# Sliding-window attention and a highway layer on one Trainium2 core: another order of loads and steps, and the gate's bias written at another place

## The chip, the core and the metric

The kernel runs on one core of a Trainium2 chip. The core has five engines that run at the same time, each with its own queue of instructions taken in order: TensorE (PE, matmuls; its weight loads are shown as PEld), VectorE (DVE), ScalarE (ACT), GpSimd (POOL) and SyncE (SP). Data comes from and goes to the chip's memory by DMA; here GpSimd issues nearly all loads and SyncE the stores. Matmul results go to PSUM, everything else is in SBUF. The metric is device time of one execution in microseconds (us), as a median of several.

## The reference

Attention with a window of 128 positions and 4 sink positions for 4 batches, 8 heads, 768 positions and a head size of 64; its output, 3072 tokens of 512 features, goes through a highway layer with two 512 x 512 weights.

```python
scores = scale * np.matmul(q, k.transpose(0, 1, 3, 2))
keep = is_sink | in_window          # pos < 4, or 0 <= query - key < 128
a = softmax(np.where(keep, scores, -1e9))
x = np.matmul(a, v)                 # then heads side by side: (3072, 512)
H = np.maximum(x @ w_h, 0.0)
T = 1.0 / (1.0 + np.exp(-(x @ w_t + b_t)))
out = T * H + (1.0 - T) * x
```

## The kernel before

**Blocks.** The 3072 tokens are 24 blocks of 128 queries, six to a batch. Keys and values are loaded in chunks of 128 that lie 64 positions off the query blocks, so block n needs key chunks n and n+1 (and n-1 for a corner) and the same of v. Chunks at a batch border are loaded in two halves.

**Steps.** Each step of a block has a short name, and the table ORDER lists them as `name:block`. All engines get their instructions in the order of this table, and what one step issues on an engine stays behind what earlier steps issued there.

- `Tq`, `Tk` (PE, L322): transposes of q and k into PSUM; `tq`, `tk` (ACT, L327): copies to SBUF; `tkV`, `tqV` the same on DVE. From block 3 on `S` carries the transposes of later blocks itself, and from block 9 one ACT copy `tt` (L334) takes both.
- `S` (PE, L375 and L388): scores of a block in two halves. `x0_`, `x1_` (ACT, L397): exp of the halves, later `xx` (L402) of both. `m0_`, `m1_`, `mm` (DVE, L408): masks.
- `sk` (PE, L357) and `es` (ACT, L364): scores and exp of the sink keys.
- `A` (PE, L441, L458, L464): the value matmuls: corners in quadrants of 64 x 64, the diagonal, and the sinks. One PSUM tile `av` serves all blocks in turn.
- `xh` (DVE, L472 and L477): division by the softmax sum. `X` (PE, L491): transposes of xh, into a free part of `av`. `xT` (ACT) or `xTV` (DVE) (L496): the copy; it must be done before `A` of the next block.
- `Mh` (PE, L519) and `Mt` (PE, L507): 4 matmuls each of 512 columns for H and for T. `u` (ACT, L512): tanh. `d` (L525), `U` (L531), `e` (L536), `o` (L548) (DVE): the rest of the layer and the store. For blocks 21 and 22 the last sum is made by GpSimd (`x2_`, `oP`). Block 23 is done in two halves of 256 columns (`Ta`, `Ha`, `ua`, `da`, `ea`, `pa` and the same with b).
- `wA` are filler matmuls on zeros; `mz`, `ma`, `na`, `mc`, `fa`, `fb`, `fc`, `fd`, `cv` are one-time set-up steps on DVE.

**PSUM.** Scores of the first blocks and all single transposes share two buffers in turn. Mh, Mt and the sink scores share two banks `m0`, `m1`; the string M_BANKS says which is used next.

**The t bias.** It is a matmul of a row of ones with the bias. For blocks 0 to 7 it is one matmul of 128 rows and 512 columns in `Mt` (L504). T_BESIDE maps a block n to the block whose bias is written in `A` of block n: from n = 9 on, two matmuls in the quadrants (low, low) and (high, high) stand ahead of the corner matmuls, which use the other two quadrants (L436). A branch for n >= LATE, which cuts them into pieces, is not used, since LATE is 99.

**Loads.** q and k of the first blocks come through one pool of 8 buffers, those of block 9 on through `late_pool` of 3; v has a ring of 14 tiles, of which 9 are used once. The first loads are written out by hand; after that `do_A` issues v of block n+4, q and k of block n+6 behind `A` of block n. `fill_ks` and `sink_v` (sink keys and values of a batch; from batch 1 on GpSimd) are issued by the copy step of the batch's first k, so they stand in GpSimd's queue behind the loads of earlier `A` steps.

Of the kernel before, what the change touches and what calls it, by code (L numbers as in the profile page):

```python
# [8 lines left out]
FP16 = mybir.dt.float16  # L9
# [11 lines left out]
def kernel(  # L21
# [37 lines left out]
    AHEAD = 8  # L59

    const = ctx.enter_context(tc.tile_pool(name="const", bufs=1))
    late_pool = ctx.enter_context(tc.tile_pool(name="p_late", bufs=3))
    sd_pool = ctx.enter_context(tc.tile_pool(name="p_sd", bufs=AHEAD))
    qkT_pool = ctx.enter_context(tc.tile_pool(name="p_qkT", bufs=7))
    tt_pool = ctx.enter_context(tc.tile_pool(name="p_tt", bufs=5))
    e_pool = ctx.enter_context(tc.tile_pool(name="p_e", bufs=3))
# [20 lines left out]

    ctx.callback(close_s)
    HP = P // 2
    T_BESIDE = {9: 8, 10: 9, 11: 10, 12: 11, 13: 12, 14: 13, 15: 14, 16: 15, 17: 16, 18: 17, 19: 18, 20: 19, 21: 20, 22: 21, 23: 22}  # L90
    LATE = 99
    M0 = 9
    FIRST = 9
    NV = FIRST + 5
    NS4 = H * NSINK
    KW = NHP * P + 32
    EW = P + HP
    v_ring = [const.tile([P, VW], FP16, tag=f"v{i}", name=f"v{i}") for i in range(NV)]
# [10 lines left out]

    def load_q(n):  # L110
        b, c = divmod(n, NSC)
        qsd = (sd_pool if n < FIRST else late_pool).tile([P, H, D], FP16, tag="qsd", name="qsd")
        nc.gpsimd.dma_start(out=qsd, in_=q[b, :, c * P:(c + 1) * P, :].transpose([1, 0, 2]))  # L113
        q_sd[n] = qsd

    def load_k(n):
        ksd = (sd_pool if n < FIRST else late_pool).tile([P, H, D], FP16, tag="ksd", name="ksd")
        for rows, b, s0 in chunk_parts(n):
            nr = rows.stop - rows.start
            nc.gpsimd.dma_start(out=ksd[rows], in_=k[b, :, s0:s0 + nr, :].transpose([1, 0, 2]))  # L120
# [69 lines left out]
    def load_w(w, sb):  # L190
        nc.gpsimd.dma_start(out=sb, in_=w.rearrange("(kc p) of -> p kc of", p=P))

    with tc.manual_schedule(engines={ENG.Pool, ENG.SP}):
        load_f32("q", 0, nc.sync)
        load_f32("k", 0, nc.scalar)
        load_f32("k", 1, nc.sync)
        load_f32("v", 0, nc.scalar)
        load_f32("v", 1, nc.sync)
        for r in (0, HP):
            nc.sync.dma_start(out=bt32[r:r + 1, :], in_=moe_b_t.unsqueeze(0))  # L200
        for b in range(B):
            nc.sync.dma_start(out=vs_dn[b], in_=v[b, :, 0:NSINK, :])
        nc.gpsimd.affine_select(
            out=ident, in_=ident, compare_op=ALU.is_equal, fill=0.0,
            base=0, pattern=[[-1, P]], channel_multiplier=1)
        tri(mask, slice(0, HP), 0, P, HP - 1, -1, 1)
        tri(mask, slice(HP, P), 0, P, 0, 1, -1)
        tri(mask, slice(0, HP), P, EW, 0, 1, -1)
        tri(mask, slice(HP, P), P, EW, -1, -1, 1)
        load_q(3)  # L210
        load_k(2)
        load_q(4)
        load_q(1)
        load_k(3)
        load_q(2)
        load_v(2)
        load_k(5)
        nc.gpsimd.affine_select(
            out=bm, in_=bm, compare_op=ALU.is_ge, fill=0.0,
            base=0, pattern=[[-NSINK, H]], channel_multiplier=1)  # L220
        nc.gpsimd.affine_select(
            out=bm, in_=bm, compare_op=ALU.is_ge, fill=0.0,
            base=NSINK - 1, pattern=[[NSINK, H]], channel_multiplier=-1)
        load_k(4)
        load_v(3)
        load_w(moe_w_h, wh_sb)
        load_q(5)
        load_k(6)
        load_w(moe_w_t, wt_sb)
        load_v(4)  # L230
        load_q(6)
        load_k(7)
        load_v(5)
        load_k(8)
        load_q(7)
        load_v(6)
        load_v(8)
        load_v(7)
# [33 lines left out]
    def sink_ones(_):  # L272
# [3 lines left out]

    m_bank = [m_ps.tile([P, DM], FP32, tag=f"m{i}", name=f"m{i}") for i in range(2)]
    M_BANKS = (
        "010101010101010101010101010010100101001100101011010110101101"
    )  # L280
    m_next = iter(M_BANKS)

# [329 lines left out]
    def on(n):  # L612
        return 0 <= n < NB
# [31 lines left out]
    def new_T(m, g):  # L645
        if g and m and m % NSC == 0 and m < NB:
            fill_ks(m // NSC, nc.gpsimd)
            sink_v(m // NSC, nc.gpsimd)

    def do_A(n):  # L650
        pe_A(n)
        if FIRST <= n + 4 <= NB:
            load_v(n + 4)
        if AHEAD <= n + 6 < NB:
            load_q(n + 6)
        if FIRST <= n + 6 <= NB:
            load_k(n + 6)

    def norm(n):
        dve_rec(n)  # L660
# [27 lines left out]
        "pa": lambda n: dve_half(n, 0, "o"), "pb": lambda n: dve_half(n, 1, "o"),  # L688
    }
    ORDER = """  # L690
    mz0_:0 ma:0 na:0 Tq:0 na:1 Tk:0 tq:0 mz1_:0 tk:0 ma:1 wA:0 wA:0 Tk:1 mc:0 cv:0 tk:1 fa:0
    wA:0 wA:0 wA:0 S:0 fb:0 x0_:0 cv:1 x1_:0 wA:0 wA:0 wA:0 wA:0 Tq:3 m0_:0 fc:0 tq:3 wA:0 Tk:2
    tk:2 m1_:0 fd:0 wA:0 wA:0 wA:0 wA:0 Tq:1 A:0 tq:1 S:1 xh:0 sk:1 x0_:1 x1_:1 Tq:2 m0_:1 X:0
    sk:3 xTV:0 es:1 Tk:3 m1_:1 tq:2 tk:3 wA:1 A:1 es:3 S:2 xh:1 x0_:2 x1_:2 Tk:4 m0_:2 sk:2
    tkV:4 X:1 es:2 m1_:2 S:3 xT:1 A:2 x0_:3 Mh:1 x1_:3 xh:2 tq:4 d:1 X:2 tk:5 Mh:0 xTV:2 m0_:3
    Mh:2 d:0 m1_:3 S:4 d:2 Mt:0 x0_:4 x1_:4 m0_:4 A:3 u:0 m1_:4 Mt:1 tq:5 xh:3 tk:6 U:0 sk:4 u:1
    e:0 S:5 es:4 o:0 X:3 x0_:5 U:1 sk:5 xTV:3 e:1 A:4 x1_:5 m0_:5 o:1 tq:6 Mt:2 tk:7 xh:4 es:5
    u:2 m1_:5 X:4 S:6 xT:4 U:2 e:2 A:5 x0_:6 o:2 Mh:3 x1_:6 xh:5 tq:7 Mh:4 m0_:6 tk:8 m1_:6 X:5
    d:3 S:7 xT:5 d:4 A:6 x0_:7 Mh:5 xh:6 x1_:7 Mt:3 d:5 tq:8 tk:9 m0_:7 X:6 u:3 m1_:7 Mt:5 xT:6
    U:3 e:3 sk:7 o:3 u:5 Tq:9 es:7 U:5 Mt:4 tq:9 e:5 o:5 S:8 u:4 U:4 A:7 x0_:8 e:4 o:4 Mt:6  # L700
    x1_:8 xh:7 tq:10 Mh:6 m0_:8 tk:10 m1_:8 u:6 X:7 d:6 S:9 xT:7 U:6 A:8 e:6 xx:9 o:6 sk:9 xh:8
    Mh:7 es:9 tt:9 mm:9 Mt:7 d:7 X:8 u:7 S:10 xTV:8 U:7 A:9 e:7 xx:10 o:7 Mt:8 xh:9 tt:10 Mh:8
    mm:10 u:8 X:9 d:8 S:11 xT:9 U:8 A:10 e:8 xx:11 o:8 sk:11 xh:10 Mt:9 es:11 tt:11 mm:11 Mh:9
    u:9 X:10 d:9 S:12 xT:10 U:9 A:11 e:9 xx:12 o:9 Mt:10 xh:11 tt:12 Mh:10 mm:12 u:10 X:11 d:10
    S:13 xT:11 U:10 A:12 e:10 xx:13 o:10 sk:13 xh:12 Mt:11 es:13 tt:13 mm:13 Mh:11 u:11 X:12
    d:11 S:14 xT:12 U:11 A:13 e:11 xx:14 o:11 Mh:12 xh:13 tt:14 Mt:12 mm:14 X:13 u:12 d:12 S:15
    xT:13 U:12 e:12 xx:15 A:14 o:12 sk:15 xh:14 Mt:13 tt:15 mm:15 es:15 X:14 S:16 u:13 xTV:14
    U:13 A:15 xx:16 Mh:14 xh:15 tt:16 Mt:14 d:14 mm:16 Mh:13 u:14 U:14 sk:17 d:13 X:15 es:17
    S:17 xT:15 e:13 e:14 A:16 xx:17 o:13 o:14 Mt:15 xh:16 tt:17 Mh:15 mm:17 u:15 X:16 S:18 d:15
    xT:16 U:15 A:17 xx:18 e:15 o:15 Mh:16 xh:17 tt:18 Mt:16 mm:18 X:17 u:16 S:19 xTV:17 d:16  # L710
    A:18 xx:19 U:16 e:16 sk:19 xh:18 Mt:17 es:19 mm:19 tt:19 Mh:17 o:16 u:17 X:18 S:20 xT:18
    d:17 U:17 A:19 xx:20 e:17 o:17 Mh:18 xh:19 tt:20 Mt:18 mm:20 X:19 u:18 S:21 xTV:19 d:18 A:20
    xx:21 U:18 e:18 sk:21 o:18 Mt:19 es:21 xh:20 tt:21 Mh:19 mm:21 u:19 X:20 S:22 d:19 xT:20
    U:19 A:21 xx:22 e:19 o:19 Mh:20 xh:21 x2_:21 tk:24 Mt:20 mm:22 X:21 u:20 S:23 xTV:21 d:20
    A:22 xx:23 U:20 e:20 sk:23 Mt:21 xh:22 x2_:22 es:23 mm:23 X:22 u:21 Mh:21 xT:22 o:20 A:23
    d:21 U:21 Mt:22 xh:23 e:21 oP:21 X:23 u:22 Mh:22 xT:23 U:22 Ta:23 d:22 Ha:23 ua:23 e:22
    oP:22 Tb:23 da:23 ea:23 Hb:23 ub:23 pa:23 db:23 eb:23 pb:23
    """

    with tc.manual_schedule(engines={ENG.PE, ENG.DVE, ENG.Activation, ENG.SP, ENG.Pool}):  # L720
# [40 lines left out]
```

## Time and profile before

| what | us |
|---|---|
| median of three runs | 120.48 (120.23 to 121.65) |
| the profiled execution | 120.48 |
| its span (first to last instruction) | 118.5 |
| TensorE busy | 106.2 |
| VectorE busy | 102.7 |
| ScalarE busy | 88.2 |
| GpSimd busy, issuing of loads counted | 78.7 |
| granted TensorE clock, mean | 0.993 |

Times in the profile count from the start of the span. A line of a timeline has the start, the length, the engine, the line of the program, the operation, its tiles, their shapes and a count; in square brackets stands how long the engine had been idle and what ended it. The difference of two starts on a busy engine, called pitch here, is what an instruction really takes of its queue: matmuls overlap, so their lengths add up to more than the time. "From issue to landing" of a load is counted from the start of the issue on GpSimd.

### The profile page before, as it was taken

The numbers are of one execution on the slowest core, as the hardware profiler recorded it, in microseconds if no ns is written. First come the engines' busy times: TensorE is split into PE (matmuls) and PEld (weight loads), VectorE is DVE, ScalarE is ACT, GpSimd is POOL, SyncE is SP. The second block draws the span as 40 slices with busy tenths as digits, with TensorE's granted clock in tenths as the row PEclk, the third lists the DMA queues.
The fourth block names the chain that finished last, engine by engine and source line by source line (L and its number), as shares of the span: only waits on it lengthen the run. The fifth ranks groups of instructions, "written<-read, shape, count | busy, mean of one in ns | idle before, by whom it ended". The sixth has DMA issues, their size and how long they took to land.

```text
span 118.5 us, 4980 instructions
## 1 busy us (share of the span) xinstructions
PE 106.2 (90%) x2119; PEld 65.2 (55%) x2119; DVE 102.7 (87%) x250; ACT 88.2 (74%) x124; POOL 78.7 (66%) x101
## 2 busy tenths in 40 slices
PE   5977787999899999999999999999999999989910
PEld 1442555546665456755666557646656675554600
DVE  6889647578999897999999999699999999999690
ACT  2447398929987969969989999869979979772410
POOL 5999976869799039976959767697692500346430
PEclk9999999999999999999999999999999999999997
DMA  2999999999999969999999999999999792201141
GB/s 60 216 173 155 145 173 175 195 155 150 121 232 205 162 84 179 180 159 184 192 182 159 145 190 168 202 135 86 221 184 164 128 160 89 89 6 78 44 180 55
DMA packets 79849, 17.65 MB, mean 149 GB/s; under 512 B 75602, under 2 KB 76882, under 8 KB 79828
## 3 DMA queue, kind: packets, MB, share of 16 engines
q0 software_dynamic: 71888, 9.97, 135.2%
q1 hardware_dynamic: 6740, 6.99, 18.9%
q10 hardware_dynamic: 1200, 0.39, 1.8%
q8 instruction: 16, 0.26, 0.9%
q14 instruction: 5, 0.04, 0.2%
HBM read 21.01 MB, written 6.29 MB: 230 GB/s over the span
## 4 chain that ended last, share of the span: by engine, by line
DVE 44%; PE 33%; DMA 6%; ACT 5%; issue 5%; POOL 3%; ACTq 0%
DVE xh L477 9%; DVE e L408 8%; DVE otok L548 7%; PE m L519 7%; DVE dd L525 6%; DMA qsd<-in_q_dram 6%; PE m L507 6%; DVE ee L536 4%; DVE u L531 4%; PE av L441 4%; PE av L458 3%; ACT e L397 3%; PE sps L322 2%; PE av L491 2%; PE sps L388 2%
## 5 line engine op out<-in xcount | busy, mean ns | idle before, releaser
L127 POOL DMA_DIRECT2D v<-in_v_dram x26 | 22.0, 849 | 13.3 <-PE av L441 10.3
L408 DVE TENSOR_TENSOR e<-e,mask 128x768 f16<-128x768 f16 (+1 forms) x33 | 24.1, 738 | 2.2 <-ACT e L397 2.2
L402 ACT ACTIVATE e<-sps,ebias 128x1536 f16<-128x1536 f32 x15 | 23.1, 1542 | 3.1 <-PE sps L388 2.8
L113 POOL DMA_DIRECT2D qsd<-in_q_dram x23 | 20.9, 910 | 5.2 <-PE sps L322 5.2
L507 PE MATMUL m<-wt_sb,xT 128*128 128x512 f16 x92 | 23.6, 379 | 0.0
L519 PE MATMUL m<-wh_sb,xT 128*128 128x512 f16 x92 | 23.3, 379 | 0.0
L120 POOL DMA_DIRECT2D ksd<-in_k_dram x26 | 22.1, 855 | 1.0 <-DVE otok L548 0.7
L397 ACT ACTIVATE e<-sps,ebias 128x768 f16<-128x768 f32 x18 | 15.3, 900 | 5.1 <-PE sps L388 4.8
L512 ACT ACTIVATE u<-m 128x512 f16<-128x512 f32 x23 | 13.7, 597 | 7.0 <-PE m L507 6.8
L477 DVE TENSOR_TENSOR xh<-av,rec 128x512 f16<-128x512 f32 x24 | 16.6, 692 | 0.8
L525 DVE SCALAR_TENSOR_TENSOR dd<-m,xh 128x512 f16<-128x512 f32 x23 | 15.7, 685 | 0.7 <-PE m L519 0.7
L548 DVE SCALAR_TENSOR_TENSOR otok<-xh,ee 128x512 f32<-128x512 f16 x21 | 14.8, 709 | 0.6
L519 PEld LDWEIGHTS <-xT 128*128 128x128 f16 x92 | 8.7, 98 | 8.6 <-issue 0.5
L507 PEld LDWEIGHTS <-xT 128*128 128x128 f16 x92 | 8.8, 98 | 8.0
L334 ACT COPY tt<-sps 128x1024 f16<-128x1024 f16 x13 | 13.0, 998 | 0.0
L327 ACT COPY t<-sps 128x512 f16<-128x512 f16 x19 | 10.4, 591 | 1.9 <-PE sps L322 1.9
L441 PE MATMUL av<-v,e 64*64 64x66 f16 x384 | 10.9, 193 | 0.7 <-DVE xT L496 0.3
L441 PEld LDWEIGHTS <-e 64*64 64x64 f16 x384 | 9.9, 107 | 3.0 <-issue 2.1
L536 DVE TENSOR_TENSOR ee<-u,dd 128x512 f16<-128x512 f16 x23 | 10.0, 439 | 0.7
L543 POOL TENSOR_SCALAR x<-xh 128x512 f16<-128x512 f16 x2 | 4.2, 2091 | 9.6 <-DVE xh L477 9.6
L458 PE MATMUL av<-v,e 128*128 128x66 f16 x192 | 10.4, 195 | 0.0
L496 ACT COPY xT<-av 128x512 f16<-128x512 f16 x16 | 9.3, 582 | 1.0 <-PE av L491 0.7
(95 smaller groups left out, 176.5 us busy)
## 6 DMA issues: line engine op xcount, KB each, us to landing
out_dram<-otok SPq DMA_DIRECT2D x23, 256.0 KB, 3.5
qsd<-in_q_dram POOLq DMA_DIRECT2D x23, 128.0 KB, 5.6
ksd<-in_k_dram POOLq DMA_DIRECT2D x19, 128.0 KB, 6.1
v<-in_v_dram POOLq DMA_DIRECT2D x19, 128.0 KB, 5.5
wh_sb<-in_moe_w_h_dram POOLq DMA_DIRECT2D x1, 512.0 KB, 8.2
wt_sb<-in_moe_w_t_dram POOLq DMA_DIRECT2D x1, 512.0 KB, 8.9
ksd<-in_k_dram POOLq DMA_DIRECT2D x7, 64.0 KB, 5.7
v<-in_v_dram POOLq DMA_DIRECT2D x7, 64.0 KB, 6.2
```

The costliest lines, as they stand in the source:

```text
L113: nc.gpsimd.dma_start(out=qsd, in_=q[b, :, c * P:(c + 1) * P, :].transpose([1, 0, 2]))
L120: nc.gpsimd.dma_start(out=ksd[rows], in_=k[b, :, s0:s0 + nr, :].transpose([1, 0, 2]))
L127: nc.gpsimd.dma_start(out=vt[rows, :, 0:D], in_=v[b, :, s0:s0 + nr, :].transpose([1, 0, 2]))
L397: nc.scalar.activation(out=e_tile(n)[:, g].rearrange("p a b c -> p a (b c)"), in_=s_tile(n, g)[:, :, 0:2 * EW], func=AF.Exp, bias=ebias, s ...
L402: nc.scalar.activation(out=e_tile(n).rearrange("p g a b c -> p (g a) (b c)"), in_=s_of[n][:, :, 0:2 * EW], func=AF.Exp, bias=ebias, scale= ...
L408: nc.vector.tensor_tensor(out=ev, in0=ev, in1=m.unsqueeze(1).to_broadcast([P, k, EW]), op=ALU.mult)
L441: nc.tensor.matmul(av[part, h // 4, h % 4, 0:_AVN], lhsT=e_at(n, h)[src, P:EW], rhs=vt[src, 65 * h:65 * h + _AVN], start=(h % 4 == 0), sto ...
L477: nc.vector.tensor_tensor(out=xh.rearrange("p (h d) -> p h d", d=D), in0=av_of.pop(n)[:, :, 0:D], in1=rec_of.pop(n).unsqueeze(2).to_broadc ...
L507: nc.tensor.matmul(t_of[n], lhsT=xT[:, kc, :], rhs=wt_sb[:, kc, :], start=False, stop=(kc == NOC - 1), skip_group_check=True)
L519: nc.tensor.matmul(hps, lhsT=xT[:, kc, :], rhs=wh_sb[:, kc, :], start=(kc == 0), stop=(kc == NOC - 1))
L525: nc.vector.scalar_tensor_tensor(out=dd, in0=h_of.pop(n), scalar=0.0, in1=xh_of[n], op0=ALU.max, op1=ALU.subtract)
L548: nc.vector.scalar_tensor_tensor(out=otok, in0=xh_of.pop(n), scalar=2.0, in1=ee_of.pop(n), op0=ALU.mult, op1=ALU.add)
```

## The change

The two pools for q and k become one of 10 buffers, the v ring has 13 tiles in a plain ring, and `do_A` of block n issues one set: q of block n+8, k and v of n+9. T_BESIDE begins at block 16, and LATE is 16, so that the bias of blocks 15 to 22 is written in four pairs of 128 columns among the corner matmuls; blocks 8 to 14 get the full bias matmul in `Mt`. The first loads stand in another order, M_BANKS and ORDER are other strings. Two copies more are on VectorE and two fewer on ScalarE; there are 6 filler matmuls more.

```diff
-    late_pool = ctx.enter_context(tc.tile_pool(name="p_late", bufs=3))
-    sd_pool = ctx.enter_context(tc.tile_pool(name="p_sd", bufs=AHEAD))
+    sd_pool = ctx.enter_context(tc.tile_pool(name="p_sd", bufs=AHEAD + 2))
...
-    T_BESIDE = {9: 8, 10: 9, 11: 10, 12: 11, 13: 12, 14: 13, 15: 14, 16: 15, 17: 16, 18: 17, 19: 18, 20: 19, 21: 20, 22: 21, 23: 22}
-    LATE = 99
+    T_BESIDE = {16: 15, 17: 16, 18: 17, 19: 18, 20: 19, 21: 20, 22: 21, 23: 22}
+    LATE = 16
...
-    FIRST = 9
-    NV = FIRST + 5
+    NV = AHEAD + 5
...
-        load_q(3)
-        load_k(2)
-        load_q(4)
-        load_q(1)
+        load_k(4)
         load_k(3)
         load_q(2)
-        load_v(2)
-        load_k(5)
         nc.gpsimd.affine_select(
             out=bm, in_=bm, compare_op=ALU.is_ge, fill=0.0,
...
-        load_k(4)
+        load_k(2)
+        load_q(1)
+        load_v(2)
+        load_q(3)
+        load_q(4)
         load_v(3)
+        load_k(5)
         load_w(moe_w_h, wh_sb)
         load_q(5)
+        load_v(4)
         load_k(6)
         load_w(moe_w_t, wt_sb)
-        load_v(4)
         load_q(6)
         load_k(7)
+        load_q(7)
         load_v(5)
         load_k(8)
-        load_q(7)
...
-        "010101010101010101010101010010100101001100101011010110101101"
+        "010100101011010101010110101010101010101010110100101001010010"
...
+    def load_set(n):
+        if on(n):
+            load_q(n)
+            load_k(n + 1)
+            load_v(n + 1)
+
     def do_A(n):
         pe_A(n)
-        if FIRST <= n + 4 <= NB:
-            load_v(n + 4)
-        if AHEAD <= n + 6 < NB:
-            load_q(n + 6)
-        if FIRST <= n + 6 <= NB:
-            load_k(n + 6)
+        load_set(n + AHEAD)
...
-    mz0_:0 ma:0 na:0 Tq:0 na:1 Tk:0 tq:0 mz1_:0 tk:0 ma:1 wA:0 wA:0 Tk:1 mc:0 cv:0 tk:1 fa:0
-    wA:0 wA:0 wA:0 S:0 fb:0 x0_:0 cv:1 x1_:0 wA:0 wA:0 wA:0 wA:0 Tq:3 m0_:0 fc:0 tq:3 wA:0 Tk:2
-    tk:2 m1_:0 fd:0 wA:0 wA:0 wA:0 wA:0 Tq:1 A:0 tq:1 S:1 xh:0 sk:1 x0_:1 x1_:1 Tq:2 m0_:1 X:0
-    sk:3 xTV:0 es:1 Tk:3 m1_:1 tq:2 tk:3 wA:1 A:1 es:3 S:2 xh:1 x0_:2 x1_:2 Tk:4 m0_:2 sk:2
-    tkV:4 X:1 es:2 m1_:2 S:3 xT:1 A:2 x0_:3 Mh:1 x1_:3 xh:2 tq:4 d:1 X:2 tk:5 Mh:0 xTV:2 m0_:3
-    Mh:2 d:0 m1_:3 S:4 d:2 Mt:0 x0_:4 x1_:4 m0_:4 A:3 u:0 m1_:4 Mt:1 tq:5 xh:3 tk:6 U:0 sk:4 u:1
+    mz0_:0 ma:0 na:0 na:1 wA:0 wA:0 Tk:0 mz1_:0 Tq:0 tk:0 fc:0 tq:0 Tk:1 fa:0 cv:0 tk:1 ma:1
+    wA:0 wA:0 wA:0 S:0 mc:0 x0_:0 cv:1 fb:0 x1_:0 m0_:0 m1_:0 fd:0 wA:0 wA:0 wA:0 wA:0 wA:0 wA:0
+    wA:0 wA:0 wA:0 wA:0 wA:0 wA:0 A:0 Tk:2 xh:0 tk:2 Tq:1 tq:1 Tk:4 tk:4 S:1 X:0 x0_:1 xTV:0
+    x1_:1 Tk:3 m0_:1 tkV:3 wA:1 Tq:3 m1_:1 sk:1 tq:3 Tq:2 es:1 tq:2 wA:1 wA:1 wA:1 S:2 A:1 x0_:2
+    sk:2 x1_:2 xh:1 es:2 m0_:2 X:1 S:3 xT:1 m1_:2 A:2 x0_:3 x1_:3 Mh:0 m0_:3 xh:2 tq:4 Mh:1 tk:5
+    d:0 X:2 m1_:3 sk:3 xT:2 S:4 d:1 es:3 A:3 x0_:4 Mh:2 x1_:4 xh:3 tq:5 Mt:2 d:2 tk:6 m0_:4 sk:4
...
-    x1_:8 xh:7 tq:10 Mh:6 m0_:8 tk:10 m1_:8 u:6 X:7 d:6 S:9 xT:7 U:6 A:8 e:6 xx:9 o:6 sk:9 xh:8
-    Mh:7 es:9 tt:9 mm:9 Mt:7 d:7 X:8 u:7 S:10 xTV:8 U:7 A:9 e:7 xx:10 o:7 Mt:8 xh:9 tt:10 Mh:8
+    x0_:8 Mt:6 x1_:8 xh:7 tq:10 m0_:8 Mt:5 tk:10 m1_:8 u:6 X:7 u:5 S:9 U:6 xTV:7 e:6 A:8 xx:9
+    U:5 e:5 o:6 Mh:7 xh:8 tt:9 sk:9 mm:9 es:9 X:8 S:10 xT:8 d:7 A:9 xx:10 o:5 sk:11 xh:9 Mh:8
+    es:11 tt:10 mm:10 Mt:7 d:8 X:9 u:7 S:11 xTV:9 U:7 A:10 xx:11 e:7 o:7 Mt:8 xh:10 tt:11 Mh:9
...
-    d:21 U:21 Mt:22 xh:23 e:21 oP:21 X:23 u:22 Mh:22 xT:23 U:22 Ta:23 d:22 Ha:23 ua:23 e:22
-    oP:22 Tb:23 da:23 ea:23 Hb:23 ub:23 pa:23 db:23 eb:23 pb:23
+    u:21 Mh:21 xT:22 o:20 A:23 d:21 U:21 Mt:22 xh:23 e:21 oP:21 X:23 u:22 Mh:22 xT:23 U:22 Tb:23
+    d:22 Ta:23 ub:23 e:22 oP:22 Ha:23 ua:23 Hb:23 da:23 db:23 ea:23 eb:23 pa:23 pb:23
```

## The prediction

> **What bounds the kernel now.** I read the busy times first, then the chain of waits, the timelines of ScalarE, TensorE and its weight loads, and GpSimd's timeline.
>
> ```profile
> span 118.5 us, 4980 instructions
> PE 106.2 (90%) x2119; PEld 65.2 (55%) x2119; DVE 102.7 (87%) x250; ACT 88.2 (74%) x124; POOL 78.7 (66%) x101
> DVE 44%; PE 33%; DMA 6%; ACT 5%; issue 5%; POOL 3%; ACTq 0%
> ```
>
> TensorE and VectorE are both near full; the chain changes between them, so neither can be dropped. Its beginning is a transfer:
>
> ```profile
> 2.80 1.05 POOL qsd L113
> 3.84 0.90 POOL ksd L120
> 4.74 0.84 POOL qsd L113
> 5.58 7.14 DMA qsd<-in_q_dram
> 12.76 0.29 PE sps L322 x8
> ```
>
> Columns: start, length. GpSimd issues q3, k2, q4, and at 5.58 q1, which lands 7.14 later; its transposes (Tq:1) run at once. On ScalarE's timeline the first exps of blocks 1, 2 and 3 follow, at 14.37, 18.32 and 21.00:
>
> ```profile
> 13.09 0.59 ACT L327 COPY t<-sps 128x512 f16<-128x512 f16 x1 [1.37 <-PE sps L322]
> 14.37 1.69 ACT L397 ACTIVATE e<-sps,ebias 128x768 f16<-128x768 f32 x2 [0.69 <-PE sps L388]
> ...
> 18.32 1.69 ACT L397 ACTIVATE e<-sps,ebias 128x768 f16<-128x768 f32 x2 [0.82 <-PE sps L388]
> ...
> 21.00 1.69 ACT L397 ACTIVATE e<-sps,ebias 128x768 f16<-128x768 f32 x2 [0.24 <-PE sps L388]
> ```
>
> On TensorE's timeline S:4 starts at 24.94, after Mh:1, Mh:0 and Mh:2 (12 matmuls of L519, 0.86 a step by the pitch):
>
> ```profile
> 21.69 1.03 PE L519 MATMUL m<-wh_sb,xT 128*128 128x512 f16 x4
> ...
> 23.11 1.90 PE L519 MATMUL m<-wh_sb,xT 128*128 128x512 f16 x8
> 24.94 0.29 PE L322 MATMUL sps<-ident,qsd 64*128 64x64 f16 x8
> ```
>
> From there TensorE has work until 112.1 (the last Hb), a stretch of about 87 us. I add its steps by pitch: 20 S at 0.82, 21 A at 0.65 with 18 sink pairs at 0.23, 21 X at 0.20, 20 Mh and 23 Mt at 0.86, 8 full biases at 0.22, sink scores 3.9, Tq:9 0.24, the last halves 1.8: 83.1, and up to 0.15 for each of 15 bias pairs beside A. So TensorE idles 2 to 4 us of 87, while VectorE, added in the same way (83.5 of 90.6 to its end at 115.57), has 7 to spare, about 2.6 of which go where its instructions are stretched beside GpSimd's tensor work (U 1.05 at 56.65, ee 1.10 at 80.42, U 0.65 at 104.31, the output 1.10 at 107.05, ee 0.80 at 113.06). TensorE's work after S:4 is what I count, with VectorE as a rival.
>
> **The start, step by step.** GpSimd now issues k4, k3, q2, the two selects on bm, k2, q1. Three issues end at 5.58 as now; the selects take 0.65 (10.04 to 10.67 now, with the gap before); k2 is issued at 6.23 and q1 at 7.10. With the measured 6.96 of k2 (3.84 to 10.80) and 7.14 of q1 they land at 13.2 and 14.24. A:0 is ready before: VectorE's steps ahead of it (fc 0.24, fa 0.92, cv:0, ma:1 0.57, mc 0.72, cv:1, fb 1.23, two masks) end near 12.4, and the 12 fillers wA:0 (0.21 each) near 10.9. If fb or cv waited they would have 0.8 us before k2.
> - q1 is 1.5 later. Then Tk:4 and its copy (tk:4, ScalarE pitch 0.52) stand ahead of S:1's second half, which needs that PSUM buffer: +0.45. First exp of block 1: about 16.3 (+1.9).
> - Block 1 to block 2: two exps 1.69, Tq:3 and its copy, es:1, tq:2, S:2: about 4.08 against 3.95 now. Three wA:1 (0.65) lie under tq:2. First exp of block 2: about 20.4 (+2.0).
> - Block 2 to S:4: A:1 now stands behind S:2, xh:1 (0.85 with rec), X:1, S:3, the mask of block 2, A:2 at +2.95, 0.9 for A:2, two Mh of 0.86, X:2 and sk:3 0.45: S:4 6.0 after the exp, against 6.62 now. S:4 near 26.35, +1.4.
> - But Mh:2 (0.86) is now behind S:4. In TensorE work the lag is **2.25**; ends 1.2 (q1 with k2 at 13.2) and 3.9 (q1 in 8.8, the slowest landing that the loads of q and k show).
>
> **The t bias.** For blocks 8 to 14 the pair beside A goes and a full L504 (0.22 in line, as 41.10 to 41.33) comes into Mt. What the pair costs now is seen in the weight loads:
>
> ```profile
> 60.59 0.12 PEld L436 LDWEIGHTS <-ones_row 64*64 64x64 f16 x2
> 60.65 0.44 PEld L441 LDWEIGHTS <-e 64*64 64x64 f16 x16
> ...
> 107.51 0.11 PEld L436 LDWEIGHTS <-ones_row 64*64 64x64 f16 x2 [0.42 <-issue]
> 107.52 0.34 PEld L441 LDWEIGHTS <-e 64*64 64x64 f16 x16
> ```
>
> At 107.5 the value weights follow 0.01 behind, at 60.6 the value matmuls are 0.14 late. So +0.07 to +0.21 a block; I take 0.10, seven blocks, +0.7. For blocks 15 to 22 two bias matmuls become eight of 128 columns among the 16 value matmuls. These pass at 0.024 each (0.38 for 16), so eight cost 0.19, or nothing if they ride in the free quadrants: between -0.14 and +0.18 against now; I take +0.06, nearer the upper end because the value matmuls' own columns would pass in less than 0.38, so issue or weight loads set their pace: eight blocks, +0.5. Together **+1.2**, ends -0.6 and +2.9.
>
> [...]
>
> **Copies, loads, end.** Two copies go from ScalarE to VectorE (tq:9 and one xT more): +0.68 on VectorE at a pitch of 0.34, nothing on the path while its 7 us of spare time cover them, 0.7 if not. Two pairs of memsets go (0.12), before 3.3 us, under the load of q0. Two rings of loads become one set of three per block, issued up to nine blocks ahead; the queue's waits for old buffers (10.3 us before v, 5.2 before q, both idle GpSimd) go and bring nothing, since TensorE waits for no q or k after 12.8. What is queued behind them is a rival below. In the last block both halves of d, e and output alternate; six instructions as now; 0 to -0.4 (the ee stretched to 0.81 beside GpSimd); I take 0.
>
> **The sum.** A later TensorE finds its inputs ready more often, so part of the 2 to 4 idle us comes back: between 0 and 2, I take 0.8, what it lost between 30 and 45 us. 2.25 + 1.2 - 0.8 = +2.65. The profiled execution took 120.48 (1.98 around its span), which is also the median; forecast **123.1**, its own range 121.6 to 124.5.
>
> **Rivals.**
> - VectorE decides from block 9 (*not slower*). From xh:9 (54.58) to its end it takes 61.0. U, e and o of block 7 move behind xh:9 (1.37), two xT copies join (0.68); its waits for TensorE in that stretch (0.93 at 77.0, 0.38 at 91.6, 0.28 at 99.4) vanish, as PE is ahead again: by A:9 it has left out Mt:7 (1.08), so the lag there is 2.25 - 1.08 - 0.7 = 0.5. 0.5 + 2.05 - 1.59 = +1.0: 121.4. It decides once TensorE's sum is 1.65 smaller than I take it, by more idle given back or a cheaper bias. For it: the chain is VectorE's from 45 to 59 and 77 to 109. Against: the added bias.
> - The bias pieces ride free and TensorE gets all its idle back (*faster than now*): 2.25 - 0.6 - 2 = -0.35: 120.1; it needs 107.52 to be the rule in every block.
> - GpSimd's fill of block 6's sink keys comes late. Now it runs here:
>
> ```profile
> 31.43 0.95 POOL L346 COPY ks<-t 64x16 f16<-64x16 f16 x2
> ```
>
>  Then 14 issues of sets 8 to 11 stand before it from about 28.1 (ten of 0.87, two pairs of halves 1.4): 39.6, and the fill is done at 40.6. TensorE reaches sk:7 at 41.4 by the same pitches. If the queue waits for transfers as between 14 and 28 us (3.3), it is 43.3, and all of TensorE stands behind sk:7 for 1.9: 125.0.
> - The lag at the start isn't there, since q1 lands as early as now: part of the low end.
>
> **The numbers.** Forecast 0.50, VectorE 0.30, late fill 0.12, free pieces 0.08. Low end 120.8 and high end 125.0 leave out about 0.1 on each side. A measurement of this kernel tells about 2% from no change, 118.07 to 122.89. Slower: 0.42 of the forecast, 0.12 of the fill, 0.05 of VectorE, 0.59; faster 0.02; within 0.39.
>
> **What would show it.** Tq:1 near 14.3, the exps of blocks 1 and 2 near 16.3 and 20.4, S:4 near 26.3: the start. Value matmuls of blocks 16 on at 0.55 to 0.60 in place of 0.38: pieces not free. ks filled by 40.6 and sk:7 without a wait: no late fill. No wait of VectorE for d after 54 us: the VectorE rival. If q1 lands before 13.2, or S:4 is under 25.5, the first step is wrong.

## The result and the profile after

The changed kernel takes 128.01 us (median of four, 127.72 to 129.22), the kernel before 120.65 beside it (four, 120.23 to 121.65): 1.062 times as long, 95% interval 1.052 to 1.071. The forecast was +2.65 us; it is +7.4. The profiled execution is the longest of the four, 129.22. Ratios here and below are to the kernel before on the same chip, with 95% intervals, and leave out executions over 1.5% above their kernel's fastest, so that some of the longest stops described below are not in them.

In this kernel every line number is 4 or 5 lower than before: S is L370 and L383, A is L436 and L453, Mt is L502, Mh is L514. The page, in the lines that answer to those of before, with the granted clock in 40 slices and the queue of instruction fetches:

```profile
span 127.2 us, 5061 instructions
...
PE 111.2 (87%) x2166; PEld 67.2 (53%) x2166; DVE 104.5 (82%) x250; ACT 87.5 (69%) x122; POOL 78.1 (61%) x101
...
PEclk9999977999999999999679999999999999999998
...
q8 instruction: 17, 0.28, 0.9%
...
DVE 54%; PE 30%; ACT 8%; issue 5%; DVEq 0%; ACTq 0%
```

TensorE is 5.0 us longer busy and its share is smaller, so it is both slower at its work and more often idle. The clock has two holes, near 17 and near 62 us. The share of VectorE in the chain has grown, which looks like the rival in which VectorE decides; the last part comes back to it. The start, on ScalarE's timeline (start, length; the first exps of blocks 1 and 2, predicted at 16.3 and 20.4):

```profile
15.95 1.69 ACT L392 ACTIVATE e<-sps,ebias 128x768 f16<-128x768 f32 x2 [0.58 <-PE sps L383]
...
21.09 1.69 ACT L392 ACTIVATE e<-sps,ebias 128x768 f16<-128x768 f32 x2 [1.51 <-PE sps L383]
```

Block 1 is a little earlier than predicted, block 2 is 0.7 late. S:4, predicted at 26.35, starts at 27.33. In the chain of waits (start, length, engine and line) two links stand out:

```profile
18.95 1.40 PE av L660 x3
...
59.59 2.28 issue
61.87 0.37 PE sps L383 x9
```

Three fillers take 1.40, where the prediction had 0.65 for them. And at 59.59 TensorE stops for 2.28 us in the middle of block 11's scores, with five of sixteen matmuls of one group done and nothing that the profile shows to wait for. TensorE's timeline shows what comes after it:

```profile
59.40 0.19 PE L383 MATMUL sps<-tt 64*64 64x64 f16 x1
61.87 0.21 PE L383 MATMUL sps<-tt 64*64 64x64 f16 x1 [2.28 <-issue]
...
63.90 1.61 PE L502 MATMUL m<-wt_sb,xT 128*128 128x512 f16 x4
65.34 1.03 PE L514 MATMUL m<-wh_sb,xT 128*128 128x512 f16 x4
```

From the start of this Mt to the start of the next step is 1.44, where such a step took 0.86 before. Busy time by windows (window, length, then busy us of PE, PEld, DVE, ACT and POOL with instructions, granted clock, share of DMA, GB/s):

```profile
14.00:18.00 4.00, 2.62 (x65) 1.59 (x65) 2.05 (x5) 3.06 (x5) 3.39 (x6) 0.91 2.37 167
18.00:22.00 4.00, 4.00 (x73) 2.35 (x69) 0.24 (x2) 2.37 (x5) 2.61 (x3) 0.66 1.97 172
...
60.00:66.00 6.00, 4.13 (x46) 2.40 (x45) 2.61 (x5) 2.84 (x3) 4.73 (x8) 0.72 1.97 170
```

Before, the window from 14 to 18 us held 3.33 busy us of TensorE at full clock:

```profile
14.00:18.00 4.00, 3.33 (x89) 2.38 (x83) 2.30 (x6) 3.13 (x6) 3.25 (x6) 1.00 2.25 170
```

The clock's own records give half speed from 17.28 to 20.69 and from 61.65 to 65.06: 3.41 us each.

What was the stop? The DMA queues of 52.6 to 59.6 us hold no packet of the instruction queue, and those of the next microsecond hold one (queue, packets, MB, share of 16 engines' time):

```profile
q0 software_dynamic: 609, 0.08, 122.9%
q1 hardware_dynamic: 100, 0.18, 47.0%
q8 instruction: 1, 0.02, 5.6%
```

It starts at 59.61, 0.02 after TensorE has run dry, and takes 0.89; work goes on at 61.87. The fetch before it was at 51.56. So it looks as if TensorE waited for its own program, which the experiments test.

The lag by blocks is best read at `xh` on VectorE, once a block. After minus before it is +2.3 us in block 9 (the prediction's steps give +0.5 there), then +4.9, +6.3, +7.7 and +8.5 in blocks 10 to 13, and +9.05 in block 23. Most of what was not foreseen comes in between 57 and 79 us, around the stop.

### The profile page after: what moved, and what is told of

It is laid out like the page before. It is cut to its first block, busy times and chain, and to the rows that moved or that the text cites. A ratio compares the mean times of both kernels' runs of the same rounds, so it can differ in the third digit from the quotient of the medians.

```text
span 127.2 us, 5061 instructions
## 1 busy us (share of the span) xinstructions
PE 111.2 (87%) x2166; PEld 67.2 (53%) x2166; DVE 104.5 (82%) x250; ACT 87.5 (69%) x122; POOL 78.1 (61%) x101
## 4 chain that ended last, share of the span: by engine, by line
DVE 54%; PE 30%; ACT 8%; issue 5%; DVEq 0%; ACTq 0%
DVE e L403 10%; DVE xh L472 10%; DVE otok L543 8%; DVE dd L520 7%; DVE ee L531 5%; DVE u L526 5%; PE m L514 5%; ACT e L392 5%; PE m L502 5%; PE m L284 3%; PE sps L317 3%; ACT t L322 2%; DVE rec L467 2%; PE av L453 2%; PE sps L383 2%
## 5 line engine op out<-in xcount | busy, mean ns | idle before, releaser
L502 PE MATMUL m<-wt_sb,xT 128*128 128x512 f16 x92 | 24.2, 386 | 0.0
L514 PE MATMUL m<-wh_sb,xT 128*128 128x512 f16 x92 | 23.4, 379 | 0.0
L507 ACT ACTIVATE u<-m 128x512 f16<-128x512 f32 x23 | 13.7, 598 | 8.1 <-PE m L502 7.9
L502 PEld LDWEIGHTS <-xT 128*128 128x128 f16 x92 | 9.1, 100 | 10.0 <-issue 2.0
L514 PEld LDWEIGHTS <-xT 128*128 128x128 f16 x92 | 8.7, 98 | 8.6 <-issue 0.4
L467 DVE RECIPROCAL rec<-av 128x8 f32<-128x8 f32 x24 | 4.9, 203 | 9.3 <-PE av L459 8.9
L322 ACT COPY t<-sps 128x512 f16<-128x512 f16 x18 | 9.9, 590 | 3.7 <-PE sps L317 3.7
L436 PE MATMUL av<-v,e 64*64 64x66 f16 x384 | 11.1, 195 | 1.3 <-DVE e L403 0.9
L436 PEld LDWEIGHTS <-e 64*64 64x64 f16 x384 | 9.8, 109 | 3.4 <-DVE e L403 1.9
L453 PE MATMUL av<-v,e 128*128 128x66 f16 x192 | 10.6, 197 | 0.0
L486 PEld LDWEIGHTS <-xh 64*128 64x128 f16 x192 | 4.1, 94 | 12.0 <-DVE xh L472 8.7
## 6 DMA issues: line engine op xcount, KB each, us to landing
qsd<-in_q_dram POOLq DMA_DIRECT2D x23, 128.0 KB, 7.1
ksd<-in_k_dram POOLq DMA_DIRECT2D x19, 128.0 KB, 7.0
v<-in_v_dram POOLq DMA_DIRECT2D x19, 128.0 KB, 7.2
```

The lines of the kernel that those rows point to most:

```text
L436: nc.tensor.matmul(av[part, h // 4, h % 4, 0:_AVN], lhsT=e_at(n, h)[src, P:EW], rhs=vt[src, 65 * h:65 * h + _AVN], start=(h % 4 == 0), sto ...
L502: nc.tensor.matmul(t_of[n], lhsT=xT[:, kc, :], rhs=wt_sb[:, kc, :], start=False, stop=(kc == NOC - 1), skip_group_check=True)
L514: nc.tensor.matmul(hps, lhsT=xT[:, kc, :], rhs=wh_sb[:, kc, :], start=(kc == 0), stop=(kc == NOC - 1))
```

## The experiments

Two theories stood against each other at first. L: loads that run up to nine blocks ahead hold up TensorE's instruction fetch. P: the stop belongs to a place in TensorE's program, and any other program would have it elsewhere or not at all.

**Loads.** `a_paced` is the changed kernel with the loads of before (two pools, ring, one v, q and k per block four and six blocks ahead); the first, hand-written list and everything else stay.

```diff
-    sd_pool = ctx.enter_context(tc.tile_pool(name="p_sd", bufs=AHEAD + 2))
+    late_pool = ctx.enter_context(tc.tile_pool(name="p_late", bufs=3))
+    sd_pool = ctx.enter_context(tc.tile_pool(name="p_sd", bufs=AHEAD))
...
-        load_set(n + AHEAD)
+        if FIRST <= n + 4 <= NB:
+            load_v(n + 4)
+        if AHEAD <= n + 6 < NB:
+            load_q(n + 6)
+        if FIRST <= n + 6 <= NB:
+            load_k(n + 6)
```

> The changed kernel with the loads of the kernel before (its two pools, its v ring, v of block n+4 and q and k of n+6 behind A of block n); the order table, the first loads and the bias stay as changed. Theory L (the loads that run ahead hold up the fetch of TensorE's instructions): the gap of 2.28 us at 59.6 goes, and the half clock after it; 122.5 to 125. Theory P (the gap belongs to the place in TensorE's program): it stays within 2 us of 59.6, 127 to 129.

It takes 124.83 us (124.69, 124.98), 1.033 [1.022, 1.043]: 3.2 less than the changed kernel. The stop is gone. The window around it, first in `a_paced` and then in the changed kernel:

```profile
58.00:80.00 22.00, 21.92 (x471) 13.50 (x473) 21.48 (x42) 18.78 (x23) 15.71 (x20) 1.00 1.60 163
```

```profile
58.00:80.00 22.00, 19.59 (x379) 11.62 (x377) 17.80 (x34) 15.20 (x19) 19.45 (x25) 0.92 2.05 173
```

The changed kernel has 2.3 busy us of TensorE less there and did fewer of its instructions. The lag of `a_paced` at `xh` grows from +2.5 in block 9 to +4.4 in block 23, not to +9.05.

`b_eager` and `b_eager2` are the other half: the kernel before with only the loads of the changed one (the same diff turned round); the two are one program, run twice.

> The kernel before with the loads of the changed one (one pool of 10, a ring of 13, a set of three loads behind each A); everything else as before. Theory L: a gap of over 1 us that TensorE spends waiting for nothing visible appears between 45 and 80 us, 122.5 to 126. Theory P: no such gap, 120 to 121.5.

> The kernel before with the changed kernel's loads alone (pools, ring, one set of three a block, issued up to nine blocks ahead), a repeat of an earlier pair of runs (122.06 and 124.04) with more rounds. The prediction has these loads at zero (the queue's waits go and bring nothing). Theory L: gaps of 1 us or more on TensorE that the profile puts to nothing, +1.5 to +3.5 us, ratio 1.012 to 1.03. Zero: ratio within 0.5% of 1.

`b_eager2` gives 1.012 [1.005, 1.019], about +1.4 us; `b_eager` took 122.06 and 124.04. TensorE's timeline of `b_eager2`:

```profile
82.24 0.22 PE L317 MATMUL sps<-ident,ksd 64*128 64x64 f16 x4
84.23 0.23 PE L317 MATMUL sps<-ident,ksd 64*128 64x64 f16 x4 [1.77 <-issue]
```

Again a group of transposes is torn in the middle for nothing visible, and another at 57.4 (1.12 between the starts). So these loads are not free on any program; but on this one they cost less than half of the 3.2. Something in the program counts as well.

**Place.** `a_shift` and `a_shift2` are the changed kernel with 12 of its early fillers cut, 512 columns into four of 128 or two of 256: the same columns, 72 or 24 more TensorE instructions. `b_shift` does the first to the kernel before, whose loads are paced.

```diff
+        if 6 <= w_seen[0] <= 17:
+            for i in range(4):
+                nc.tensor.matmul(t[:, 128 * i:128 * i + 128], lhsT=warm[:, 0:P],
+                                 rhs=warm[:, 128 * i:128 * i + 128], start=True, stop=True)
+            return
         nc.tensor.matmul(t, lhsT=warm[:, 0:P], rhs=warm, start=True, stop=True)
```

> The changed kernel, the 12 filler matmuls of 512 columns ahead of A:0 cut into 48 of 128 columns: the same columns, 72 TensorE instructions more ahead of everything that follows. Theory P: the gap moves 72 instructions (about 1.5 us) earlier in the work, or goes, then 123 to 125. Theory L: a gap of 2 us or more stays between 55 and 65 us, 127 to 129. Both: the half clock at 17 to 21 us stays or is a little longer.

> The changed kernel with 12 early fillers cut into two of 256 columns: 24 TensorE instructions more, the loads still running ahead. Place alone (theory P): the gap stays at the same border (the 1984th instruction) or vanishes, with no new ones. Fetch held up by loads and met at a border (L with borders): one or more gaps of 0.9 to 2.3 us again, at 192 plus multiples of 256, between 14 and 79 us, while loads flow, none over 0.9 after 79 us; time 125.5 to 128.5.

> The kernel before with 12 of its early fillers of 512 columns cut into 48 of 128: 36 matmuls and their weight loads more (72 instructions), the same columns, its loads paced as before. It shifts every later instruction of TensorE within its program. Theory P (a gap belongs to a place in TensorE's program and to how its blocks of instructions fall): gaps of 1 us or more appear somewhere and the time rises by 1 to 2 us. Theory L (gaps need loads that run ahead of the work): no gap over 0.8 us that the profile puts to nothing, time within 0.5 us of before.

`a_shift`: 126.63 (126.55, 126.71), 1.048 [1.037, 1.058]; the stop at 59.6 is gone and one of 1.66 stands at 63.3. `a_shift2`: 126.40, 1.048 [1.038, 1.058], with a stop of 1.44 at 64.3 and none over 0.9 once the loads have ended. With the same loads the three places of the borders thus give 128.0, 126.6 and 126.4. `b_shift`: 122.24 (121.74 to 123.40), 1.014 [1.008, 1.021], where L had foreseen a time within 0.5 us of before and P +1 to +2 us. TensorE's timelines of `a_shift2` and then of `b_shift`:

```profile
64.18 0.33 PE L453 MATMUL av<-v,e 128*128 128x66 f16 x5
65.76 0.26 PE L453 MATMUL av<-v,e 128*128 128x66 f16 x3 [1.25 <-issue]
```

```profile
30.27 0.24 PE L388 MATMUL sps<-t,t 64*64 64x64 f16 x5
31.43 0.28 PE L388 MATMUL sps<-t,t 64*64 64x64 f16 x11 [0.91 <-issue]
```

Neither theory stands alone. They join when all records of TensorE are counted in order of start: matmuls, weight loads, and the semaphore and drain records of its sequencer (45 in the changed kernel), without which the numbers below don't line up. All stops of 0.87 us or more (between two starts) for which the fetch, and no wait, fits:

| kernel | stop at instruction | at us | stop | fetch begun before work resumed |
|---|---|---|---|---|
| changed | 1984 | 59.4 | 2.48 | 2.26 |
| a_shift | 1216, 2240, 3008 | 36.8, 63.3, 83.1 | 0.91, 1.66, 0.87 | 3.19, 2.50, 2.35 |
| a_shift2 | 2240 | 64.3 | 1.44 | 2.44 |
| b_shift | 704, 960 | 21.8, 30.3 | 1.17, 1.10 | 2.42, 3.26 |
| b_eager | 448, 3008 | 18.8, 83.0 | 1.29, 1.36 | 2.42, 2.44 |
| b_eager2 | 1984, 3008 | 57.4, 82.3 | 1.12, 1.96 | 2.40, 2.70 |
| p_start | 960 | 33.5 | 2.10 | 2.95 |
| p_warm | 1984, 3520 | 58.3, 94.6 | 1.73, 1.91 | 3.60, 2.25 |
| p_q1 | 960, 1216 | 34.5, 41.4 | 1.00, 0.87 | 2.91, 2.59 |
| p_bias | 960 | 33.9 | 1.48 | 3.52 |
| b_pieces | 2496 | 69.6 | 1.02 | 2.69 |
| p_warm2, p_warm4 | 960, 960 | 31.1, 30.9 | 1.10, 0.98 | 3.36, 3.20 |
| before, a_paced, p_all, b_t16p | none | | | |

For 18 of the 20 the profile has "issue" as the releaser, and no other stop of this length has it; for two (`a_shift` 3008, `p_warm2` 960) it names a step of ScalarE. Every one of these instruction numbers is 192 plus a multiple of 256, in kernels whose programs differ, and the page's 0.28 MB in 17 packets is 16.5 KB a packet. In these runs the program thus comes in blocks of 256 instructions, with as many fetches as borders: 17 packets and 17 borders in the changed kernel, 16 and 16 before. Paired in order, the first fetch with the first border, each is read here as bringing what stands behind the next border: the changed kernel passed border 1728 at 54.1, the fetch began 5.5 later, border 1984 was reached at 59.4, and work went on 2.26 after the fetch had begun. At the 20 stops work resumed 2.25 to 3.60 us after that, and the borders without a stop agree: at 269 borders in the 17 profiled executions, paired in this way, TensorE never went on earlier than 2.25 us after the fetch began. When does that fetch begin? Counted from the moment at which TensorE passes (at a stop, reaches) its border, over the six borders from 1472 to 2752 (some 45 to 81 us), on average: before 1.7 us, `a_paced` 1.2, the changed kernel 3.3, `b_eager` 3.9, `b_eager2` 3.5. In the changed kernel at the five borders from 3008 on, when no load is under way (the last landed before 86), it is 0.3; two of its 17 fetches, at 68.66 and 99.12, begin 0.8 and 1.3 ahead of their borders. At the five borders up to 1216 (some 10 to 42 us) it is 2.6 to 4.7 in all 17 executions, and there stand 8 of the 11 stops of kernels with paced loads, both of `b_shift` among them. So loads that run ahead make the fetch late (L), and which border is reached too soon depends on what lies between two borders (P). Where in the DMA queues the fetch is held was not seen: the trace does not tell which of the 16 engines carries it.

A stop does not always cost its length. In `b_shift` the lag at `xh` goes from -0.3 in block 2 to +1.7 in block 6, a little under the sum of its two stops, 2.3. But the stop of 1.10 at 31 us in `p_warm2` cost about 0.1: its lag in block 9 is +1.53, that of `p_warm`, which has no such stop before 58 us, +1.44. And stops differ between executions: `b_eager` and `b_eager2` are one program, with stops at 448 and 3008 in one profile and at 1984 and 3008 in the other.

**The bias.** `b_pieces` is the kernel before with LATE = 16, `b_t16p` with T_BESIDE from 16 too (and a string M_BANKS to fit): the changed kernel's bias alone. `p_bias` puts the bias of before into `a_paced`; there, by the order table and its string M_BANKS, the t biases of blocks 8 to 10 are overwritten by H matmuls before they are used, though all their matmuls run.

```diff
-    T_BESIDE = {9: 8, 10: 9, 11: 10, 12: 11, 13: 12, 14: 13, 15: 14, 16: 15, 17: 16, 18: 17, 19: 18, 20: 19, 21: 20, 22: 21, 23: 22}
-    LATE = 99
+    T_BESIDE = {16: 15, 17: 16, 18: 17, 19: 18, 20: 19, 21: 20, 22: 21, 23: 22}
+    LATE = 16
```

> The kernel before with LATE = 16 alone: the bias of blocks 15 to 22 in four pairs of 128 columns among the corner matmuls. By the step of the prediction (0.06 us a block) the corner matmuls take 0.55 in place of 0.38 and 0.14 ahead of them goes: 120.5 to 121.5. If the pieces ride free: 119.3 to 120.3. [...]

> The kernel before with the changed kernel's t bias alone: no pair beside the value matmuls of blocks 9 to 15, a full bias in Mt there, and pieces from block 16. The prediction's step is +1.2 us (0.7 for blocks 8 to 14, 0.5 for the pieces, ends -0.6 and +2.9), less what TensorE's 2 to 4 idle us take back; the pieces alone measured +0.35. Sum theory: +0.4 to +1.2 us, ratio 1.003 to 1.010. [...]

> The run before with the loads paced as before (a_paced, 124.8), and now also the bias of blocks 8 to 22 in pairs ahead of the corner matmuls from block 9 on, as before (each bank as in the changed kernel). If what a_paced loses between blocks 11 and 13 (1.8 us) is the added bias: 123.4 to 124.2 and half of it gone. If it is Mt:7, which stands behind A:9 (1.08 us of TensorE): under 0.5 gone, 124.3 to 125.

`b_pieces` is 1.003 [0.998, 1.008], `b_t16p` 1.0039 [1.0002, 1.0076]: the whole bias costs +0.5 us (0.0 to 0.9). `p_bias` is 125.65 (125.29 to 126.42), 0.8 over `a_paced` and not under it, with a fetch stop of its own at instruction 960 (1.48) and three blocks whose matmuls share a bank otherwise than planned; it can't size the bias. The pieces themselves, on TensorE's timeline of the changed kernel, in block 16:

```profile
89.05 0.22 PE L436 MATMUL av<-v,e 64*64 64x66 f16 x2
89.05 0.24 PE L443 MATMUL m<-bt,ones_row 64*64 64x128 f16 x2
...
89.27 0.22 PE L436 MATMUL av<-v,e 64*64 64x66 f16 x3
89.43 0.43 PE L453 MATMUL av<-v,e 128*128 128x66 f16 x8
```

From the first corner matmul to the next group it takes 0.38 with eight bias pieces in between, as it took 0.38 without them; in all eight blocks from 16 on it is 0.36 to 0.38. The pieces ride free. Yet `b_pieces` is not faster, where 119.3 to 120.3 was expected if they ride free, and in its profile the lag stays at +2.1 from block 15 to block 23. The 0.14 that TensorE saves in most of these blocks (0.38 in place of 0.52) brings nothing.

**Where q1 lands.** `p_q1` is `a_paced` with k2 and q1 ahead of k4, k3 and q2; `p_start` keeps three issues ahead of the selects on bm.

```diff
+        load_k(2)
+        load_q(1)
         load_k(4)
-        load_k(3)
-        load_q(2)
...
-        load_k(2)
-        load_q(1)
+        load_k(3)
+        load_q(2)
```

(This is `p_start`; `p_q1` only moves the first two lines up.)

> a_paced with k2 and q1 at the head of GpSimd's queue, ahead of k4, k3 and q2. If the place of q1 in the queue makes the start late: Tq:1 right behind A:0 (12.8), exps of block 1 near 15, of block 2 near 19.8, block 4 on at least 1 us earlier, 123.3 to 124. If the start is late through the order and the clock: 124.5 to 125.

> The changed kernel with the loads of before (as a_paced), and at the start the same three issues ahead of the two selects on bm, but k2, q1, k4 in place of k4, k3, q2 (k3 and q2 follow the selects). The selects stay where they are, which the earlier run with k2 and q1 first didn't keep. If q1's landing sets the start (the prediction's first step): q1 lands near 12.7, Tq:1 near 13, the exps of block 1 near 15, S:4 1 to 1.5 us earlier than in a_paced (27.7), and the time 1 to 1.5 under a_paced, 123.3 to 123.8. If instead A:0 and the order table behind it set it: exps of block 1 near 16 still, and no gain. The clock: TensorE's idle spots before Tq:1 shrink by about a us, so its half-clock stretch (15 to 22 in a_paced) may shorten too; then up to 0.8 more.

`p_q1` is slower, 127.19 (125.71 to 127.23), 1.053 [1.041, 1.065]: the selects go behind five issues, VectorE waits 1.2 for bm, and A:0 and all behind it are later. It changed two things, which `p_start` mends: 1.031 [1.025, 1.038], so no gain on `a_paced` that can be told, though q1 lands at 10.4 in place of 13.7. TensorE's timeline of `p_start`:

```profile
13.57 0.28 PE L322 MATMUL sps<-ident,qsd 64*128 64x64 f16 x8
14.41 0.29 PE L322 MATMUL sps<-ident,ksd 64*128 64x64 f16 x8 [0.56 <-ACT t L327]
14.90 0.29 PE L375 MATMUL sps<-t,t 64*128 64x128 f16 x4 [0.20 <-ACT t L327]
15.39 0.29 PE L375 MATMUL sps<-t,t 64*128 64x128 f16 x4 [0.20 <-ACT t L327]
```

Tq:1 no longer waits for q1, and S:1 still has its second half at 15.39, against 15.42 in the changed kernel: three waits for ScalarE's copies stand in line behind A:0, Tk:2 and Tq:1, in the order that the table sets. The exps of block 1 come at 15.91, as in `a_paced`, and S:4 at 27.36. The order, not the landing, makes the start late.

**The clock.** `p_warm` is `a_paced` with nine fillers of 512 columns more in the idle spots of the start; in `p_warm2` and `p_warm4` six of them are cut into two and four, which leaves the work alone and moves the borders. `p_all` has the fillers, q1 as in `p_q1` and the bias as in `p_bias` (with the same three biases lost).

```diff
-    wA:0 wA:0 wA:0 wA:0 wA:0 wA:0 A:0 Tk:2 xh:0 tk:2 Tq:1 tq:1 Tk:4 tk:4 S:1 X:0 x0_:1 xTV:0
-    x1_:1 Tk:3 m0_:1 tkV:3 wA:1 Tq:3 m1_:1 sk:1 tq:3 Tq:2 es:1 tq:2 wA:1 wA:1 wA:1 S:2 A:1 x0_:2
+    wA:0 wA:0 wA:0 wA:0 wA:0 wA:0 wA:0 wA:0 wA:0 A:0 Tk:2 xh:0 tk:2 wM:1 Tq:1 tq:1 Tk:4 tk:4 wM:1 wM:1 S:1 X:0 x0_:1 xTV:0
+    x1_:1 wM:1 wM:1 wM:1 Tk:3 m0_:1 tkV:3 wA:1 Tq:3 m1_:1 sk:1 tq:3 Tq:2 es:1 tq:2 wA:1 wA:1 wA:1 S:2 A:1 x0_:2
```

> a_paced with nine more filler matmuls in TensorE's idle spots between 11 and 17 us (three ahead of A:0, six on a free bank around S:1). If the idle spots bring the clock down: it stays at 1.00 from 15 to 22 us, the exps of block 2 come 0.7 to 1.2 us earlier, 123.5 to 124.2. If not, 124.5 to 125.5, since the fillers stand in the queue.

> a_paced with all three: bias of before, k2 and q1 first, nine fillers more. If the three terms are what is left, 121 to 122.5; if the order table itself is slower, 123 or more.

> The paced changed kernel with nine fillers at the start (as p_warm), six of them cut into two of 256 columns: the same columns, 12 TensorE instructions more than p_warm, so every border of 256 instructions falls 12 earlier in the work. Clock theory: no half clock at 14 to 22 us, block 4's scores (S:4) near 26.3 as predicted, and where no gap over 0.8 us stands, the time is 1.4 under a_paced (124.83): 123.4. If the clock's 1.4 us is taken back later anyway (VectorE or another wait then ends last): S:4 near 26.3 and still 124.3 or more without a gap. A gap at a border costs its length on top of either.

> The same with the six fillers cut into four of 128 columns: 36 TensorE instructions more than p_warm. Clock theory as for p_warm2: S:4 near 26.3, 123.4 without gaps. Border theory for both: their gaps of 0.9 us and more, if any, stand at instruction 192 plus a multiple of 256, each ending 2.3 to 3.3 us after a fetch began, and the times of p_warm, p_warm2 and p_warm4 differ by the sums of their gaps, up to 3 us, though they do the same work.

The clock lines of the pages of `a_paced` and of `p_warm2`:

```profile
PEclk9999955999999999999999999999999999999997
```

```profile
PEclk9999999999999999999999999999999999999999
```

In `a_paced` TensorE ran at half speed from 14.98 to 21.80; with the fillers it doesn't, and S:4 starts at 26.27 (`p_warm2`), 26.28 (`p_warm`) and 26.32 (`p_warm4`) in place of 27.74. The predicted 26.35 holds, given a full clock. Times: `p_warm` 1.032 [1.024, 1.039], `p_warm2` 123.83 (123.20 to 124.99), 1.028 [1.018, 1.038], `p_warm4` 124.61 (124.00 to 125.13), 1.033 [1.025, 1.041]. These can't be told from `a_paced`. The lag at `xh` in the profiled executions says where the 1.4 us went: `p_warm2` is 1.4 ahead of `a_paced` in block 3, 0.9 in blocks 4 to 17 (`p_warm`, with no stop there, 1.0 in blocks 4 and 9), and 0.4 in block 23, after another stop of 0.75 at a border (3520). So about a third is taken back at once by other waits, some 1.0 is carried, and part of that goes in a stop. For the executions that were not profiled this is only argued. `p_all` has neither half clock nor stop and takes 125.47 (124.47 to 125.66), the branch "the order table itself is slower"; its start is that of `p_q1` (S:4 at 27.25).

Some profiled executions are the longest of their kernel, and have large stops: `p_warm` 128.54 (others 123.89 and 124.31) with 3.64 us of stops, `p_start` 126.14 (others 124.01 to 125.12) with 2.10, `b_eager2` 123.95 (others 121.44 to 123.02) with 3.08. What stops the others had was not recorded.

## Why the prediction was wrong

**Bound: right up to block 13, not behind it.** After 54 us VectorE waits for TensorE in the changed kernel:

```profile
DVE rec L467 <- PE av L459: 3.8, 2, 2.8
DVE dd L520 <- PE m L514: 0.9, 1, 0.9
```

(line waited for, total, times, longest). The rival in which VectorE decides from block 9 needed these waits to vanish; the longest one is VectorE behind TensorE's stop at 59.6. So that rival is not what made the kernel slower. But from about 72 us on the chain is nearly all VectorE's, VectorE is busy 6.9 to 7.8 of every 8 us, the lag hardly grows (+8.5 in block 13, +9.05 in block 23), and `b_pieces` shows that less TensorE work there brings nothing. Counting TensorE's work to the end, as the sum does, is not borne out for these blocks; that VectorE is the bound there is argued, since no run makes its work less.

**Loads: the step that failed.** The queue's waits for old buffers were to "go and bring nothing, since TensorE waits for no q or k after 12.8". The second half is true, and the term, put at zero, is +3.2 us (128.01 against 124.83). The step asked which data TensorE waits for, and not what else the loads hold up: here the fetch of TensorE's own program, which began 3.3 us after a border on average over the six borders from 1472 to 2752, and 1.2 in `a_paced`. The size belongs to where the borders fall: the same loads cost 1.4 us on the old order. In the profiled execution the stop and the half clock behind it make up to 2.3 + 1.7 = 4.0 us (half speed for 3.41 us loses at most half of that).

**The clock: an assumption unsaid.** The steps of the start were priced at full clock. The half-speed stretch moves S:4 from 26.27 to 27.33 in the changed kernel and to 27.74 in `a_paced`, +1.06 and +1.47 at that point; of the 1.47 about 1.0 is left in block 9 (+2.47 in `a_paced`, +1.44 in `p_warm`). The prediction counted idle on TensorE at the start as free.

**The start: times right, cause wrong.** Tq:1 came at 13.96 (14.3 predicted), the exps of block 1 at 15.95 (16.3), S:4 at 26.27 with a full clock (26.35). With Mh:2 behind it that is 1.33 + 0.86 = 2.2 of lag, 2.25 predicted. But `p_start` shows that an earlier q1 doesn't bring it back: the chain of copies behind A:0 takes as long. The rival "q1 lands as early as now" would not have been the low end.

**Bias and idle: two errors against each other.** The bias is +0.5, not +1.2, the pieces free. That issue or weight loads set the pace of the value matmuls, the author's reason for +0.06 a block, is shown by no run: eight pieces with eight weight loads of their own among them left the corner matmuls at 0.36 to 0.38. The 0.8 of idle given back is not seen: in `p_warm`, which has full clock and no stop before 58 us, the lag of 2.2 at S:4 is +1.4 at `xh` of block 9, 2.5 with Mt:7 (1.08) owed there, where the prediction had 0.5 and 1.6; in block 13 it is +3.3 (`p_warm2`). The idle itself was also misread: the last Hb runs from 112.47 to about 112.9, not to 112.1, so by its own sum TensorE idled 3 to 5 us.

**Late fill: no.** GpSimd was 1.1 later than reckoned, and TensorE was later too. From GpSimd's and TensorE's timelines:

```profile
41.21 0.48 POOL L341 COPY ks<-t 64x16 f16<-64x16 f16 x2
...
43.12 0.62 PE L352 MATMUL m<-t,ks 128*128 128x128 f16 x8
```

The fill is done at 41.69 and sk:7 doesn't wait for it. (The late case of the rival should read 43.9 by its own figures, 40.6 + 3.3, not 43.3.)

**End: right.** From `xh` of block 23 to the end of the span it takes 9.02 us against 9.40 before, within the 0 to -0.4 given.

**The account.** The profiled execution of the changed kernel is 8.74 over that of before (129.22 and 120.48). 4.53 of this is its distance to `a_paced` (124.69): the lag grows from +2.3 to +8.5 between blocks 9 and 13 in the one and from +2.5 to +4.3 in the other, so the loads, through the stop and the half clock behind it. Of the 4.21 that are left, about 1.0 is the half clock at the start. The remaining 3.2 stand against the forecast of 2.65, inside its range of 121.6 to 124.5. That it comes so near owes something to luck, since the bias was too dear by 0.7 and the idle given back too large by about as much. Of the 3.2, 1.7 come between blocks 11 and 13 in `a_paced` and in `p_warm2` alike; what share of that is the Mt:7 owed (1.08) was not tested.

## What to carry to other kernels

Loads that ran further ahead held up the fetch of an engine's program here (3.3 to 3.9 us after a border on average, against 1.2 and 1.7 with paced loads): when a wait of the load queue goes, ask what was let through in the meantime, not only who waited for the data. An engine that stops in the middle of a group of like instructions, with "issue" as the only releaser, as for 2.28 us at 59.59, should be looked up against the instruction queue's packets (one began at 59.61); a few dummy instructions that shift the program tell such a stop from one that belongs to the work (in `a_shift` it was gone, and one of 1.66 stood at 63.3). And idle spots on TensorE at the start are not free if they bring the clock down, as in `a_paced` (busy 2.67 of 4 us from 14 to 18, half speed from 14.98 to 21.80): price the steps behind them at half speed. Filling them brought the scores of block 4 forward by 1.4 us here, but no gain in the whole time that can be told.

## What was not expected of the hardware

- TensorE's program came in blocks of 256 instructions: all 20 stops in the table above stand at 192 plus a multiple of 256, and the changed kernel has 17 such borders and 17 packets of 16.5 KB in its instruction queue. A stop at a border lasted up to 2.48 us.
- 36 more matmuls on zeros, with the same columns, made the kernel before 1.4% slower (`b_shift`).
- The half-speed stretches at 17.28 and 61.65 in the changed kernel are 3.41 us long, that at 14.98 in `a_paced` is 6.83, about twice as much. Idle of 2.28 us at 59.59 was followed by half speed from 61.65, and idle of only 1.69 us at 94.83 in `p_warm` by half speed from 96.95, while idle of 1.77 (`b_eager2`) and 1.91 (`p_start`) was not. At the start of the changed kernel half speed came with TensorE busy 2.62 of 4 us (14 to 18) and no gap over 0.9 us. So in these runs the length of one gap does not decide.
